# Another order of the first 42 feed-forward tasks in a fused attention and feed-forward kernel, with filler products in more places

## The chip, the cores and the metric

The kernel runs on one core of a Trainium2 chip. The metric is the device time of one execution in microseconds (us), as a median of several runs.

## What is computed

A recurrent attention (RWKV) runs over 4 batches, 8 heads and 768 positions with head size 48. Its output, 3072 tokens of 384 numbers, goes through two matrix products with a gelu between them.

```python
def _attn_ref(r, k, v, w, u):
    for t in range(S):
        kt, vt, rt, wt = (k[:, :, t], v[:, :, t], r[:, :, t], w[:, :, t])
        cur = np.einsum('bhd,bhe->bhde', u[None] * kt, vt)
        y[:, :, t] = np.einsum('bhd,bhde->bhe', rt, state + cur)
        state = wt[:, :, :, None] * state + np.einsum('bhd,bhe->bhde', kt, vt)
...
def _moe_ref(x, w_in, w_out):
    h = x @ w_in                                  # 3072x384 by 384x2048
    g = h * (1.0 / (1.0 + np.exp(-1.702 * h)))
    return (g @ w_out).astype(np.float32)         # 2048x384
```

## The kernel before

The 3072 tokens are 24 chunks of 128 (six for each batch). The attention of one chunk is a Python generator, `chunk(t)`, that is run in 13 steps. The feed-forward part is 6 groups of 4 chunks. A task is one group (or, for the first group's early tasks, half of it) with one of the 16 slices of the hidden dimension.

All instructions are issued in an order that is written out by hand: `RAMP` is a string of tokens, `do(token)` runs one token, and each engine gets its instructions in that order. An engine works its own list from front to back, so an instruction that must wait holds back all that stand behind it on the same engine. `RAMP` holds everything up to task 41; from task 42 on a fixed rule (`rest`) sets the order. The tokens are:

- `a5` runs the next step of chunk 5. This text calls them a5.1 to a5.13. Steps 1 to 3 are VectorE scans and the product `kq` (lines 330 to 341); 4 is four TensorE transposes and a ScalarE copy; 5 is `rku` on VectorE (line 356; line 359 to 361 from chunk 8 on); 6 is small TensorE products (`ps_d`, line 368) and 7 the ScalarE scaling of `am` from them; 8 is the TensorE products `ps_u`; 9 is the state update (lines 406 to 412); 10 the masked copies into `am` (line 415), which also give two PSUM banks back; 11 and 12 the TensorE products `ps_y` with a one-element copy between them (line 448); 13 moves `ps_y` into `x`, the input of the feed-forward part.
- `l5` issues loads of chunk 5, `m5` squares a scan's result on ScalarE (line 277), `f3` issues the load of weight piece 3, and `w3` runs one of four steps of its conversion: two ScalarE passes, two VectorE passes (lines 256 and 259), the high part on ScalarE, the low part on VectorE (line 267, tiles `l0` to `l11`).
- `g9`, `h9`, `y9` are task 9: first product (TensorE, tile `ph`), gelu (two ScalarE passes, then `gl` on VectorE, line 522), second product (TensorE, tiles `po`, line 540 to 542; the third of each three matmuls reads `gl`). Tasks 0 to 4 use one fp32 product in place of three (lines 497 and 537) and need only the first two conversion steps.
- `x1` copies attention rows into the third block of `x` of the first two chunks by six small DMAs (line 481), three from SyncE's queue and three from GpSimd's. `g0` reads them.
- `d6` sets 6 filler products: 128x512 bf16 matmuls of a constant tile `warm` with itself (line 305). They are issued by the next token that takes a PSUM bank, into that bank, ahead of its own work.

There are five banks for `bank(name)`, handed out in the order in which they were given back.

```python
BANKS = 5
...
def bank(name):
    i = free.pop(0)
    x = ps_a.tile([P, WIDE], F32, tag=f"bank{i}", name=name)
    while cold:
        times, n = cold.pop()
        for _ in range(times):
            T.matmul(..., warm, warm_b[:, 0:n], start=True, stop=True)
```

## Time and profile before

| | us |
|---|---|
| median of three runs | 501.91 (501.61 to 502.9) |
| span of the profiled execution, first to last instruction | 501.6 |
| TensorE busy | 489.3 (98%) |
| VectorE busy | 294.2 (59%) |
| ScalarE busy | 227.2 (45%) |

The profiled execution's own device time is not listed apart from the span. The median lies 0.3 us above the span, and the text takes these 0.3 us as what lies around it. Busy shares are means over the whole run. The VectorE and ScalarE work of the attention and of the weight conversion lies in the first third, where all three engines are close to full.

### The profile page before, as it was taken

The page shows a single profiled execution, that of the slowest core. Times are in us where ns is not written, and L with a number is a line of the kernel's source. Part 1 is how long each engine was busy: PE and PEld are TensorE (multiplying, and loading weights), DVE is VectorE, ACT ScalarE, POOL GpSimd, SP SyncE. Part 2 cuts the span into 40 slices and gives each one's busy share as a digit, 9 for nine tenths or more (in the row PEclk, how much of TensorE's full clock was granted, in tenths as well). Part 3 has the DMA queues.
Part 4 walks back from the last instruction along what each step waited for, and adds up shares of the span by engine and source line. Part 5 has one row for each costly group of instructions (what it writes and reads, how often), then busy time and mean ns, then how long its engine had stood idle before and what let it go on. Part 6 is the DMA issues. An engine that isn't in the chain of part 4 may idle for free.

```text
span 501.6 us, 11866 instructions
## 1 busy us (share of the span) xinstructions
PE 489.3 (98%) x5036; PEld 405.8 (81%) x5036; DVE 294.2 (59%) x502; ACT 227.2 (45%) x526; POOL 15.4 (3%) x48
## 2 busy tenths in 40 slices
PE   8989999999999999999999999999999999999996
PEld 4668999887887888888888888888888878888884
DVE  8889999989898314765655555655655521111211
ACT  2889899775444324432342442342442332322221
POOL 2001000001001000000001000001000001000000
PEclk9989999999999999999999999999999999999999
DMA  7884988056532500261104171104040001100001
GB/s 200 259 214 138 221 263 226 23 151 185 173 83 55 136 0 3 95 190 48 48 3 126 45 208 49 51 1 126 23 138 1 1 1 31 64 0 0 1 0 70
DMA packets 26508, 45.82 MB, mean 91 GB/s; under 512 B 3952, under 2 KB 17712, under 8 KB 26448
## 3 DMA queue, kind: packets, MB, share of 16 engines
q1 hardware_dynamic: 25472, 42.94, 30.5%
q0 software_dynamic: 864, 1.66, 1.4%
q8 instruction: 41, 0.67, 0.6%
q10 hardware_dynamic: 112, 0.39, 0.3%
q14 instruction: 19, 0.16, 0.1%
HBM read 38.00 MB, written 4.72 MB: 85 GB/s over the span
## 4 chain that ended last, share of the span: by engine, by line
PE 87%; DVE 8%; DMA 2%; issue 1%; ACT 1%; SPq 0%; DVEq 0%; ACTq 0%
PE po L540 12%; PE ph L502 12%; PE ph L504 12%; PE ph L503 12%; PE po L542 12%; PE po L541 12%; PE ps_y L438 2%; PE ps_y L425 2%; PE ps_u L402 2%; PE ph L497 2%; PE ps_u L398 2%; DMA wkr_t<-in_wkr 2%; PE ps_t L348 2%; PE po L537 1%; DVE lp L330 1%
## 5 line engine op out<-in xcount | busy, mean ns | idle before, releaser
L522 DVE TENSOR_TENSOR gl<-gf,gh 128x512 fp32r<-128x512 f32 (+1 forms) x101 | 65.7, 650 | 158.2 <-ACT gf L520 157.2
L519 ACT ACTIVATE gh<-ph 128x512 fp32r<-128x512 f32 (+1 forms) x101 | 57.1, 566 | 204.9 <-PE ph L504 193.8
L502 PE MATMUL ph<-x,h 128*128 128x512 f32 (+1 forms) x303 | 115.6, 382 | 0.7 <-DVE am L415 0.7
L504 PE MATMUL ph<-x,l 128*128 128x512 f32 (+1 forms) x303 | 113.4, 374 | 0.0
L540 PE MATMUL po<-gh,h 128*128 128x512 f32 (+1 forms) x297 | 113.3, 381 | 0.0
L503 PE MATMUL ph<-x,h 128*128 128x512 f32 (+1 forms) x303 | 113.2, 373 | 0.0
L542 PE MATMUL po<-gl,h 128*128 128x512 f32 (+1 forms) x297 | 111.2, 374 | 1.2 <-DVE gl L522 1.2
L541 PE MATMUL po<-gh,l 128*128 128x512 f32 (+1 forms) x297 | 110.9, 374 | 0.0
L502 PEld LDWEIGHTS ph<-x,h 128*128 128x128 f32 x303 | 57.0, 188 | 10.8 <-PE po L542 0.9
L542 PEld LDWEIGHTS po<-gl,h 128*128 128x128 f32 x297 | 55.9, 188 | 12.0 <-DVE gl L522 1.9
L504 PEld LDWEIGHTS ph<-x,l 128*128 128x128 f32 x303 | 57.0, 188 | 10.4
L503 PEld LDWEIGHTS ph<-x,h 128*128 128x128 f32 x303 | 57.1, 188 | 9.6
L540 PEld LDWEIGHTS po<-gh,h 128*128 128x128 f32 x297 | 55.9, 188 | 10.4
L541 PEld LDWEIGHTS po<-gh,l 128*128 128x128 f32 x297 | 56.0, 188 | 9.3
L520 ACT ACTIVATE gf<-ph 128x512 f32<-128x512 f32 (+1 forms) x101 | 56.7, 562 | 4.6 <-DVE gl L522 4.6
L330 DVE TENSOR_TENSOR_SCAN lp<-wkr_t,d1r 112x516 f32<-112x516 f32 x24 | 29.4, 1226 | 1.0 <-DMA wkr_t<-in_wkr 1.0
L341 DVE TENSOR_TENSOR kq<-wkr_t,lp 112x1024 f32<-112x1024 f32 x24 | 29.3, 1221 | 0.9 <-PE ps_y L438 0.6
L335 DVE TENSOR_TENSOR_SCAN lp<-wkr_t,d1f 112x516 f32<-112x516 f32 x24 | 29.5, 1229 | 0.5
L350 ACT COPY kt<-ps_t 128x448 f32<-128x448 f32 (+1 forms) x24 | 12.7, 530 | 34.4 <-PE ps_t L348 34.4
L277 ACT ACTIVATE junk<-lp 112x1032 bf16<-112x1032 f32 x24 | 25.5, 1063 | 0.0
L438 PE MATMUL ps_y<-kq,mid 64*64 64x64 f32 (+3 forms) x384 | 22.9, 218 | 0.8 <-ACT mid L448 0.4
L481 POOL DMA_DIRECT2D x<-x x18 | 9.0, 507 | 380.1 <-DVE x L272 269.2
(101 smaller groups left out, 517.5 us busy)
## 6 DMA issues: line engine op xcount, KB each, us to landing
st<-in_w_out SPq DMA_DIRECT2D x6, 1024.0 KB, 6.0
rk_t<-in_vrk SPq DMA_DIRECT2D x16, 384.0 KB, 4.3
st<-in_w_in SPq DMA_DIRECT2D x6, 896.0 KB, 8.6
v_t<-in_vrk SPq DMA_DIRECT2D x24, 192.0 KB, 3.7
out_t<-ob SPq DMA_DIRECT2D x15, 256.0 KB, 2.3
wkr_t<-in_wkr SPq DMA_DIRECT2D x18, 192.0 KB, 3.2
wkr_t<-in_wkr SPq DMA_DIRECT2D x36, 96.0 KB, 3.4
wkr_t<-in_wkr SPq DMA_DIRECT2D x5, 577.9 KB, 4.8
```

The source lines that it names most:

```text
L330: V.tensor_tensor_scan(li[:, ::-1], w1[:, ::-1], d1r.rearrange("r p c -> r (p c)")[:, ::-1], 0.0, op0=ALU.mult, op1=ALU.add)
L335: V.tensor_tensor_scan(pm, w0, d1f.rearrange("r p c -> r (p c)"), 0.0, op0=ALU.mult, op1=ALU.add)
L438: T.matmul(ps[b][head(h), p], from_[head(half), p * D + OFF * h : p * D + HB], qf[head(half), p, blocks[b]], start=False, stop=p == PAIRS[ ...
L502: T.matmul(ph, h_, xs[i][:, 0, c, cs], start=c == 0, stop=False)
L503: T.matmul(ph, h_, xs[i][:, 1, c, cs], start=False, stop=False)
L504: T.matmul(ph, l_, xs[i][:, 0, c, cs], start=False, stop=c == NM - 1)
L519: A.activation(gh, ph, AF.Gelu_apprx_sigmoid, scale=1.0 / W_SCALE)
L520: A.activation(gf, ph, AF.Gelu_apprx_sigmoid, scale=1.0 / W_SCALE)
L522: V.tensor_tensor(gl, gf, gh.bitcast(F32), op=ALU.subtract)
L540: T.matmul(o, h_, gh, start=first, stop=False, skip_group_check=True)
L541: T.matmul(o, l_, gh, start=False, stop=False, skip_group_check=True)
L542: T.matmul(o, h_, gl, start=False, stop=f == NF - 1, skip_group_check=True)
```

## The change

Only the string `RAMP` changes. Of its tokens other than the fillers each one occurs as often as before, so the work of every engine is the same; the place of many of them is another. The filler products go from 52 in 6 groups to 78 in 12 groups (14 tokens; two of the groups are filled by two tokens). What `rest` issues from task 42 on is the same. The first lines:

```diff
 RAMP = """
-l0 M l1 l0 a0 a0 a0 d26 a0 l0 a1 a0 d6 a0 f0 m0 a0 a0 l2 a1 l1 a1 l2 a0 a1 m1 a1 d6 a1 l3 a1 a0 a2 a1 a0 a1 a0 a1 w0
-l3 a2 a1 a0 a2 a3 d5 a2 a1 a1 f1 w1 f2 x1 a2 a3 d4 a2 a3 a2 a2 l4 a3 a2 a3 d5 a3 w0 f3 a3 a3 a2 a3 m2 a3 g0 h0 g1 w2
...
+d31 l0 a0 l1 a0 l0 a0 a0 m0 M a0 d3 a1 l0 a1 a0 a0 f0 l2 a1 d3 a0 d5 a0 a1 m1 d6 l2 a1 l1 a0 a2 a1 d3 a1 a1 a2 a1 a0
+a0 d5 l3 a2 a1 w0 d3 a2 a0 f1 f2 a1 d4 a1 d2 a3 l3 a2 a3 w1 a1 a2 x1 d4 l4 a2 a2 a3 a3 d5 w0 a3 a3 m2 a3 d3 g0 a2 a2
+a3 g1 f3 w1 h0 d1 l4 a3 w2 a3 a2 w2 h1 a2 f4 a2 a3 a4 g2 w3 a3 y0 w3 w2 y1 w0 a3 g3 g4 h2 h3 f5 w3 y2 h4 w0 y3 s0 y4
...
```

The number of filler products ahead of each piece of work, in TensorE's order, was 26 (transposes a0.4), 6 (a0.6), 6 (a1.6), 5 (a2.4), 4 (a2.6), 5 (a3.6). It is now 31 (a0.4), 3 (a0.6), 3 (a0.8), 5 (a1.4), 6 (a1.6), 3 (a1.8), 8 (a2.4), 6 (a2.6), 4 (a2.8), 5 (a3.6), 3 (`g0`) and 1 (a2.11).

TensorE around the first feed-forward product, before. `ps_d` is a3.6, `ps_u_527` and `ps_u_528` are a3.8, the six `ph` matmuls are `g0` and `g1` (three fp32 products each), and `ps_y_586` is a2.11.

```order
L368 MATMUL ps_d<-hm,rku 128x2 x4
L398 MATMUL ps_u_527<-v_t_84,kt 64x48
L398 MATMUL ps_u_527<-v_t_84,kt 48x48
...
L402 MATMUL ps_u_528<-kq 64x64
L497 MATMUL ph<-l_384,l_351 128x256 x6
L425 MATMUL ps_y_586<-am,v_t_86 48x64
```

The same place in the changed kernel, where a3.8 is `ps_u_558` and `ps_u_559`:

```order
L368 MATMUL ps_d<-hm,rku 128x2 x4
L305 LDWEIGHTS warm
L305 MATMUL ph<-warm 128x512
...
L497 MATMUL ph<-l_386,l_367 128x256 x3
L398 MATMUL ps_u_558<-v_t_84,kt 64x48
...
L402 MATMUL ps_u_559<-kq 64x64
L402 MATMUL ps_u_558<-kq 64x64
L497 MATMUL ph<-l_386,l_367 128x256 x3
```

`g0` now stands ahead of a3.8, behind three fillers, and a3.8 stands between `g0` and `g1`.

VectorE around the low part of weight piece 6 (`l6`, conversion step w6.4), before. `h11` with `st_844` is w6.2, `sf` and `mid` are a4.9, `am` is a4.10, `rku` a5.5, the `gl` rows are the tasks 12 and 13, and `st_857` with `h10` is w7.2.

```order
L259 SCALAR_TENSOR_TENSOR h11_952<-h11_952,st_844 128x1024
L522 TENSOR_TENSOR gl_1033<-gf_1031,gh_1032 128x256
...
L412 TENSOR_TENSOR sf1_88<-ps_u1_878,mid0_90 112x192
L267 TENSOR_TENSOR l6_1042<-h11_952,h6_1037 128x1024
L415 COPY_PREDICATED am_867<-after_102,ps_u0_877 128x256
...
L356 TENSOR_TENSOR rku_1063<-wkr_t1_83 112x512
L522 TENSOR_TENSOR gl_1077<-gf_1075,gh_1076 128x256
L256 SCALAR_TENSOR_TENSOR st_857<-st_857 128x1024
L259 SCALAR_TENSOR_TENSOR h10_1028<-h10_1028,st_857 128x1024
```

The same place in the changed kernel, where the `gl` rows are the tasks 12, 13 and 14 and `st_864` is w7.2's:

```order
L259 SCALAR_TENSOR_TENSOR h11_941<-h11_941,st_856 128x1024
...
L412 TENSOR_TENSOR sf1_88<-ps_u1_958,mid0_90 112x192
L522 TENSOR_TENSOR gl_1072<-gf_1070,gh_1071 128x256
L415 COPY_PREDICATED am_891<-after_102,ps_u0_957 128x256
...
L522 TENSOR_TENSOR gl_1127<-gf_1125,gh_1126 128x256
L356 TENSOR_TENSOR rku_1132<-wkr_t1_83 112x512
L522 TENSOR_TENSOR gl_1136<-gf_1134,gh_1135 128x256
L256 SCALAR_TENSOR_TENSOR st_864<-st_864 128x1024
L259 SCALAR_TENSOR_TENSOR h10_1055<-h10_1055,st_864 128x1024
L267 TENSOR_TENSOR l6_1150<-h11_941,h6_1102 128x1024
```

`l6` moved back past a4.10, a5.5, the whole of w7.2 and one more `gl`.

VectorE around the `gl` of task 25, the last of the first group, before. `am` is a8.7, `x` is a7.13, `lp` is a9.2 and `kq` a9.3.

```order
L383 TENSOR_TENSOR am<-same,s 128x256 x2
L272 TENSOR_TENSOR x<-ps_y_1771,x 112x4x64
L272 TENSOR_TENSOR x<-ps_y_1772,x 112x4x64
L335 SCALAR_TENSOR_TENSOR lp<-wkr_t_83,d1f 112x516
L341 TENSOR_TENSOR kq<-wkr_t_83,lp 112x1024
L522 TENSOR_TENSOR gl<-gf,gh 128x512
L359 TENSOR_TENSOR rk_t<-rk_t 128x384
```

The same place in the changed kernel (lines 408 to 412 are a8.9):

```order
L383 TENSOR_TENSOR am<-same,s 128x256 x2
L272 TENSOR_TENSOR x<-ps_y_1802,x 112x4x64
L272 TENSOR_TENSOR x<-ps_y_1803,x 112x4x64
L335 SCALAR_TENSOR_TENSOR lp<-wkr_t_83,d1f 112x516
L522 TENSOR_TENSOR gl<-gf,gh 128x512
L408 TENSOR_TENSOR sf_88<-sf_88,lp 112x192
...
L341 TENSOR_TENSOR kq<-wkr_t_83,lp 112x1024
```

The product `kq` of a9.3 went behind `gl` and behind a8.9.

## Rows read from the trace of the kernel before

**Rows 1.** The page: busy us, share of the span and instructions of each engine.

```profile
PE 489.3 (98%) x5036; PEld 405.8 (81%) x5036; DVE 294.2 (59%) x502; ACT 227.2 (45%) x526; POOL 15.4 (3%) x48
```

**Rows 2.** Stretches of 20 us: length, busy of five engines, granted clock, DMA share, GB/s.

```profile
60.00:80.00 20.00, 19.32 (x199) 18.96 (x199) 19.24 (x28) 17.93 (x43) 0.00 (x0) 1.00 0.74 222
...
180.00:200.00 20.00, 20.00 (x151) 16.50 (x150) 5.40 (x10) 5.58 (x11) 0.00 (x0) 1.00 0.01 1
```

**Rows 3.** Short stretches around the first feed-forward products, same columns.

```profile
26.00:28.00 2.00, 1.57 (x26) 0.94 (x15) 1.79 (x5) 1.97 (x6) 0.18 (x1) 1.00 1.13 212
28.00:30.00 2.00, 1.38 (x10) 0.97 (x8) 1.97 (x3) 2.00 (x9) 0.00 (x0) 1.00 1.05 215
...
31.00:32.00 1.00, 0.67 (x20) 0.51 (x13) 0.90 (x4) 1.00 (x5) 0.00 (x0) 0.93 0.91 113
32.00:33.00 1.00, 1.00 (x4) 0.82 (x3) 0.90 (x4) 1.00 (x2) 0.00 (x0) 0.50 0.45 162
...
35.00:36.00 1.00, 1.00 (x5) 0.64 (x3) 0.62 (x1) 1.00 (x2) 0.00 (x0) 0.86 0.65 224
```

**Rows 4.** TensorE (PEld: weight loads) in order of time: start, length, instruction, idle before.

```profile
1.14 7.46 PE L305 MATMUL ps_t<-warm 128*128 128x512 bf16 x26 [1.14 <-DVE warm L119]
...
4.53 3.57 PEld L305 LDWEIGHTS <-warm 128*128 128x128 bf16 x17 [0.28 <-issue]
...
9.39 0.57 PE L348 MATMUL ps_t<-ident,kq 112*128 112x112 f32 x4 [0.79 <-DVE kq L341]
...
19.24 0.68 PE L438 MATMUL ps_y<-kq,mid 64*64 64x64 f32 x8 [0.36 <-ACT mid L448]
...
31.62 4.51 PE L497 MATMUL ph<-l,l 128*128 128x256 f32 x12 [0.33 <-DVE am L415]
36.06 0.69 PE L425 MATMUL ps_y<-am,v_t 64*48 64x64 f32 x32
```

**Rows 5.** VectorE's first long wait, in a0.9.

```profile
14.84 0.36 DVE L412 TENSOR_TENSOR sf<-ps_u,mid 112x192 f32<-112x192 f32 x1 [1.25 <-ACT mid L406]
```

**Rows 6.** The DMAs of `x1`: issue; then KB each and median us to landing.

```profile
24.30 1.88 SPq L481 DMA_DIRECT2D l<-l  x3
...
x<-x SPq DMA_DIRECT2D x3, 32.0 KB, 2.3
l<-l SPq DMA_DIRECT2D x3, 16.0 KB, 6.5
```

**Rows 7.** TensorE in order of time: its waits behind 36 us, and some neighbours.

```profile
72.67 0.36 PE L502 MATMUL ph<-x,h 128*128 128x256 f32 x1 [0.68 <-DVE am L415]
...
75.77 0.39 PE L502 MATMUL ph<-x,h 128*128 128x256 f32 x1
...
81.37 0.28 PE L540 MATMUL po<-gh,h 128*128 128x256 f32 x1
81.49 0.28 PE L541 MATMUL po<-gh,l 128*128 128x256 f32 x1
82.09 0.39 PE L542 MATMUL po<-gl,h 128*128 128x256 f32 x1 [0.32 <-DVE gl L522]
...
123.19 0.39 PE L541 MATMUL po<-gh,l 128*128 128x512 f32 x1
124.49 0.50 PE L542 MATMUL po<-gl,h 128*128 128x512 f32 x1 [0.91 <-DVE gl L522]
...
153.18 0.69 PE L425 MATMUL ps_y<-am,v_t 64*48 64x64 f32 x32 [0.46 <-DVE am L415]
```

**Rows 8.** VectorE in order of time.

```profile
74.93 1.22 DVE L259 SCALAR_TENSOR_TENSOR h<-h,st 128x1024 int32<-128x1024 int32 x1
...
122.61 1.23 DVE L341 TENSOR_TENSOR kq<-wkr_t,lp 112x1024 f32<-112x1024 f32 x1
```

**Rows 9.** Waits of VectorE between 36 and 165 us: total, times, longest.

```profile
DVE mid L409 <- PE ps_u L402: 2.1, 3, 1.1
DVE mid L448 <- PE ps_y L438: 1.6, 2, 1.1
```

## The prediction

> **What bounds the kernel now.** I read the page first. TensorE is busy for 489.3 of 501.6 us, VectorE for 294.2 and ScalarE for 227.2 [rows 1]. So TensorE's list sets the end, and there are two ways to gain: fewer instructions in it, or less time in which it waits or runs slowly. The change adds instructions (26 fillers), so it can only gain by the second.

> The 20 us stretches say where that time lies. From 180 to 200 us TensorE has no gap (20.00 of 20.00) and VectorE is idle for three quarters. From 60 to 80 us TensorE misses 0.68 us, and VectorE (19.24) and ScalarE (17.93) are nearly full [rows 2]. So the first 160 us are a three-engine relay with little room, and what follows is TensorE alone. All tokens are the same but the fillers, so what is won or lost up to task 42 arrives at the end one for one.

> The busy share hides something. From 32 to 33 us TensorE counts as busy for 1.00 of 1.00 at a granted clock of 0.50, the lower of its two levels; the fall begins within the row from 31 us (0.93) and ends within the one from 35 us (0.86), with two more rows at 0.50 between [rows 3]. The loss is 0.07 + 3 x 0.50 + 0.14 = 1.7 us, and the 12 fp32 matmuls of `g0` and `g1` pay it: 4.44 us from their start at 31.62 to the next row at 36.06 [rows 4]. Ahead of the fall TensorE was busy for only 1.57 and 1.38 of 2 us, and 0.67 of 1 [rows 3].

> Then I listed the waits of TensorE behind 36 us. There are four of size: task 15's first product at 72.67 (released by the masked copy of a4.10, which gives its PSUM bank back), `y16` at 82.09 and `y25` at 124.49 (both for `gl`), and a11.11 at 153.18 (for a11.10) [rows 7]. The idle column is too small, since a matmul of 0.28 us is followed by the next after 0.12 (81.37, 81.49): `y16` lost 82.09 - 81.49 - 0.12 = 0.48, and by the same 0.16 task 15 lost 0.68 + 0.16 = 0.84 and `y25` 0.91 + 0.16 = 1.07 (from 123.19 to 124.49 less 0.23). For a11.11 I keep the 0.46 of its row. Together 2.85 us.

> **The change, part by part.** *Start.* A filler costs 3.57 / 17 = 0.21 us at the full clock [rows 4]. The first 26 run from 1.14 to 8.60, and the transposes a0.4 start at 9.39 after 0.79 of idle time for `kq`. Five more end 5 x 0.21 = 1.05 later, at about 9.65 by the last one's end; a next instruction overlaps that end by 0.16, so a0.4 starts at about 9.5, 0.1 late. Against that, `rku` of a0.5 now stands ahead of chunk 1's scan on VectorE, so a0.6 need not wait for it, ScalarE gets through a0.7 about 0.6 earlier, and VectorE's wait in a0.9 (1.25 us at 14.84 [rows 5]) falls to about 0.6. Then the fillers ahead of a0.8, a1.4, a1.6 and a1.8 come (17 in place of 6, 2.3 us), of which the relay hides most. I walked TensorE's list with the durations of the same steps in this trace and get a0.12 at 19.7 in place of 19.24 [rows 4]: 0.5 late.

> *To the first feed-forward products.* From a0.12 to a2.11 both orders hold the same real work of TensorE. Fillers in it go from 14 to 27: 13 x 0.21 = 2.8 us. They lie where TensorE was idle (0.43, 0.62 and 0.33 us in the three rows from 26 to 32 us, 1.4 in sum [rows 3]), and if they keep the clock up, 1.7 us of slow running go. By this account a2.11 moves by +0.5 + 2.8 - 1.4 - 1.7 = +0.2 us. The walk along the chain gives more, because idle time ahead of 26 us is filled too and a3.8 moves between `g0` and `g1`: a3.6 at 30.2, three fillers, `g0` at 31.85, a3.8 at 33.15, `g1` at 34.1, one filler, a2.11 at 35.65 in place of 36.06, that is -0.4. I take -0.4, since the walk sees the waits one by one, and keep +0.2 as the other end.

> *Task 15's wait.* In the bank list of the new order task 15 gets the bank of a5.4, which ScalarE frees early; a4.10's goes to a5.6. The 0.84 go.

> *A new wait.* `g16` is the first product that reads `l6`, in its third matmul. TensorE has the same real work ahead of `g16` in both orders, so it arrives there at 75.77 [rows 7] - 0.84 - 0.4 = 74.5 and wants `l6` at 74.8. VectorE now makes `l6` behind w7.2, which ended at 74.93 + 1.22 = 76.15 [rows 8] with `l6` already counted ahead of it; with one more `gl` (0.42 like any of that width, less 0.1 of overlap) and 0.4 of lead that is 76.1. Cost: 1.3 us. This is the price of moving `l6` back; its bounds are 0 (if VectorE gains an earlier start from its shorter waits) and 1.7 (no lead).

> *`y16`.* Two more first products and `h17` now lie ahead of it, 18 matmuls at 0.12 or 2.2 us of cover for `gl` of task 16. The 0.48 go.

> *`y25`.* The `kq` of a9.3 (1.23 us at 122.61 [rows 8]) no longer stands ahead of `gl`, which is then ready 1.2 us earlier, about when TensorE asks. The 1.07 go. Its transposes a9.4 are late by the same amount, but they now stand behind `g26`, which covers them.

> *a11.11.* It no longer follows a10.11 directly; feed-forward products lie between. The 0.46 go.

> Sum: -0.4 - 0.84 + 1.3 - 0.48 - 1.07 - 0.46 = -1.95 us, from 501.6 to 499.65 in span, and with the 0.3 us between span and median 499.9 us. Moves of loads I cost at nothing: no chunk load or weight piece is asked for later by more than it was early, and SyncE's weight loads of pieces 1 and 2 now stand ahead of a load that had to wait.

> [...]

> **The rivals.** *The waits come back elsewhere, or the clock falls all the same.* VectorE has 0.76 us free between 60 and 80 us [rows 2]. A TensorE that is 2 us earlier asks for `gl` earlier, and a product that now just makes it will wait. If the clock also falls at some other gap, 1.7 us go again. With either of these 499.9 becomes about 501.6. For it: the tight engines; against it: at the two hand-overs that I checked VectorE's own order became better.

> *VectorE gains too.* Between 36 and 165 us it waits 2.1 us for `ps_u` and 1.6 us for the copy of line 448, both for TensorE [rows 9], because products of the attention stand behind feed-forward products. The new order puts several of them ahead (a8.11 ahead of `y26`). If half of these 3.7 us goes, and TensorE is held by VectorE there, another 1.9 us go: 498.0.

> *Slower: the DMAs of `x1` come late.* a1.13 now stands behind a weight conversion on ScalarE, so `x1` is issued at about 27.1, 2.8 us later than 24.30 [rows 6]. Three issues take 1.88, so the last leaves some 1.3 after the first. With the 6.5 us to landing that they took then, the last lands at 34.9, while the last third of `g0` wants it at 31.85 + 0.86 = 32.7. TensorE waits 2.2 us, and the idle time brings the fall of the clock (1.7): 499.9 + 3.9 = 503.8. With the 2.3 us of the later `x` copies [rows 6] it lands at 30.7 and nothing waits. It decides at 4.3 us to landing. Against it: the 2 MB of weight pieces that those DMAs shared the queues with are now asked for earlier.

> **How the numbers follow.** As summed (499.9): 0.42, with a range of its own from 498.7 to 501.2. VectorE gains too (498.0): 0.17. Waits or the slow clock come back (501.6): 0.24. Late `x1` (503.8): 0.17. A measurement of this kernel can tell about 0.3%, 1.5 us, from no change: faster is below 500.4, slower above 503.4. Of the first case three quarters lie below 500.4 (0.32), which with the second and a little of the third gives 0.52 for faster; late `x1` is slower in most of its cases (0.14); 0.34 is left for no change. The range leaves out 2 in 10: the far half of the second case and most of the late `x1`, so 497.5 to 502.8.

> **What would show it.** Right: a granted clock of 1.00 from 5 us on; a0.12 near 19.7, `g0` near 31.9 and a2.11 near 35.7; no wait at task 15, `y16` and `y25`; a wait of about 1.3 us of `g16`'s third matmul for VectorE's line 267; task 42's first product about 2 us earlier. Wrong: `g0` waiting for the DMAs of line 481, a clock of 0.50 in any stretch, or new TensorE waits for line 522 that add up to what the four old ones cost.

## The result and the profile after

| | us |
|---|---|
| before, median of 6 runs | 502.27 (501.61 to 502.9) |
| changed, median of 6 runs | 508.02 (506.46 to 511.18) |
| ratio, with 95% interval | 1.0112, [1.0086, 1.0139] |
| span of the profiled execution | 509.5, its own time 511.18: the slowest of the six |

The change makes the kernel slower by 1.1%, about 5.7 us, where 499.9 was forecast. A run's time is 1.7 us above its span, not 0.3 as I had reckoned. So before's profiled execution, with its span of 501.6, took about 503.3 us and was some 1.0 above before's median; the changed kernel's was 3.2 above its own.

The changed kernel's page, answering [rows 1], and TensorE in order of time, answering [rows 4]:

```profile
PE 498.2 (98%) x5062; PEld 409.5 (80%) x5062; DVE 294.4 (58%) x502; ACT 227.0 (45%) x526; POOL 15.4 (3%) x48
```

```profile
19.78 0.67 PE L438 MATMUL ps_y<-kq,mid 64*64 64x64 f32 x8 [0.24 <-ACT mid L448]
...
32.56 1.46 PE L497 MATMUL ph<-l,l 128*128 128x256 f32 x6
...
35.03 1.56 PE L497 MATMUL ph<-l,l 128*128 128x256 f32 x6
...
36.74 0.46 PE L425 MATMUL ps_y<-am,v_t 64*48 64x64 f32 x16
...
41.30 0.27 PE L438 MATMUL ps_y<-kq,sf 64*64 64x64 f32 x1 [2.01 <-issue]
```

a0.12 is where the walk had it (19.78 against 19.7). Against the walk `g0` is 0.7 late (32.56 for 31.85) and a2.11 is 1.1 late (36.74 for 35.65). The fall of the clock at `g0` and `g1` is gone. Then comes something that no row of before has: at 41.30, in the middle of a3.11, TensorE had stood for 2.01 us and waited for nothing that the trace names. Such a gap, ended by `issue` in the rows, is called a stop below. Behind it the clock falls; the short stretches, as [rows 3]:

```profile
42.00:43.00 1.00, 1.00 (x3) 0.83 (x4) 0.51 (x2) 0.97 (x2) 0.00 (x0) 0.58 1.06 246
43.00:44.00 1.00, 1.00 (x4) 0.72 (x3) 0.00 (x0) 1.00 (x2) 0.00 (x0) 0.50 1.06 143
...
121.00:122.00 1.00, 1.00 (x5) 0.90 (x4) 0.90 (x4) 1.00 (x6) 0.00 (x0) 0.50 1.06 317
```

There are two falls of 3.4 us ahead of the end in this execution, from 42.2 and from 120.7 us, with 1.7 us lost in each. The second has no stop in front of it. What `g0` has ahead of it shows on ScalarE (`w1.1` is the row of L253, a1.13 those of L462 behind it):

```profile
23.86 0.13 ACT L448 COPY mid<-ps_y 1x1 f32<-1x1 f32 x1
26.80 1.20 ACT L253 ACTIVATE st<-st 128x1024 int32<-128x1024 uint32 x1 [2.81 <-DMA st<-in_w_out]
27.88 1.20 ACT L254 ACTIVATE h<-st 128x1024 f32<-128x1024 f32 x1
...
29.04 0.39 ACT L462 ACTIVATE l<-ps_y 112x256 f32<-112x256 f32 x1
```

The load of piece 1 was issued at 15.49 in place of 18.91, and `w1.1` got it 1.5 us later than before (26.80 against 25.25). a1.13 waits behind it, and `x1` is issued at 29.92. The DMAs from SyncE's queue then landed in 1.9 us (median), not in 6.5 [rows 6]:

```profile
29.92 1.89 SPq L481 DMA_DIRECT2D l<-l  x3
```

```profile
l<-l SPq DMA_DIRECT2D x3, 16.0 KB, 1.9
```

The waits of TensorE from 36 to 165 us that the view lists (total, times, longest); the four of [rows 7] are gone, but for 0.2 us of L542:

```profile
PE ps_y L438 <- issue: 2.0, 1, 2.0
PE ps_y L438 <- ACT mid L448: 0.8, 3, 0.3
PE ph L504 <- DVE l L267: 0.4, 1, 0.4
PE po L542 <- DVE gl L522: 0.2, 1, 0.2
```

**Where the time went.** For each trace I took the start of every real matmul of TensorE (no filler) and subtracted the real work before it, each matmul at the median interval to the next one that its line and shape have in before. What is left is lost: waits, fillers, slow clock. It is given when 18, 70, 90, 130 and 200 us of real work are done (in before at 43, 99, 121, 166 and 239 us). The rows e1 to e14 are experiments of the next section; each row is one execution.

```
lost, us            18    70    90   130   200
before            24.9  28.6  31.3  36.2  38.5
changed           30.2  33.8  39.7  44.0  46.3
e1  same again    27.4  30.9  36.8  41.1  43.4
e3                25.2  31.4  36.9  40.6  42.9
e4                25.2  28.8  32.8  37.1  39.4
e5                24.5  26.7  29.7  34.5  36.8
e9                28.4  32.0  37.8  41.5  43.8
e10               26.4  30.0  35.5  39.8  42.0
e14               26.1  29.8  33.7  38.0  40.2
```

Of the 7.8 us between the two profiled executions 5.3 arise in the first stretch and 3.2 in the third, 0.6 come back in the fourth. From 18 to 70 both orders lose the same (3.7 and 3.6). In the first stretch 0.7 are there by a2.11 (36.74 against 36.06); the stop (2.0) and the fall behind it (1.7) make most of the rest. In the third the second fall makes 1.7, and waits that no row of before has make 1.2 (`Not seen at all`, below).

### The profile page after: what moved, and what is told of

It is laid out like the page before. It is cut to its first block, busy times and chain, and to the rows that moved or that the text cites. A ratio compares the mean times of both kernels' runs of the same rounds, so it can differ in the third digit from the quotient of the medians.

```text
span 509.5 us, 11912 instructions
## 1 busy us (share of the span) xinstructions
PE 498.2 (98%) x5062; PEld 409.5 (80%) x5062; DVE 294.4 (58%) x502; ACT 227.0 (45%) x526; POOL 15.4 (3%) x48
## 4 chain that ended last, share of the span: by engine, by line
PE 89%; ACT 4%; DVE 2%; DMA 2%; issue 2%; ACTq 0%
PE po L540 13%; PE ph L502 12%; PE ph L504 12%; PE po L542 12%; PE po L541 12%; PE ph L503 12%; PE ps_y L438 3%; PE ps_y L425 2%; DMA st<-in_w_out 2%; PE ps_u L402 2%; PE ps_u L398 2%; PE ps_t L305 2%; PE ps_t L348 2%; ACT am L378 1%; PE po L564 1%
## 5 line engine op out<-in xcount | busy, mean ns | idle before, releaser
L542 PE MATMUL po<-gl,h 128*128 128x512 f32 (+1 forms) x297 | 111.5, 376 | 0.2 <-DVE gl L522 0.2
L542 PEld LDWEIGHTS po<-gl,h 128*128 128x128 f32 x297 | 56.2, 189 | 10.6 <-DVE gl L522 0.4
L438 PE MATMUL ps_y<-kq,mid 64*64 64x64 f32 (+3 forms) x384 | 24.3, 221 | 1.6 <-ACT mid L448 1.3
L438 PEld LDWEIGHTS ps_y<-kq,mid 48*48 48x48 f32 (+3 forms) x384 | 19.2, 129 | 4.8 <-ACT mid L448 2.0
```

The source lines that it names most:

```text
L438: T.matmul(ps[b][head(h), p], from_[head(half), p * D + OFF * h : p * D + HB], qf[head(half), p, blocks[b]], start=False, stop=p == PAIRS[ ...
L542: T.matmul(o, h_, gl, start=False, stop=f == NF - 1, skip_group_check=True)
```

## The experiments

The first theories: A, the load of piece 1 lands late and holds ScalarE, with `x1` and `g0` behind it; B, the 26 fillers lie on TensorE's path; C, the loss is made by the later order; D, stops and falls of the clock. Ratios are against runs of before beside each group of experiments, on the same chip; before's median there was 503.15 (e1 to e4), 502.48 (e5 to e8), 503.42 (e9 to e12) and 503.17 (e13 to e16).

**e1: the changed kernel again.** 

> The changed kernel as it is, for a second profile. The first one has two stretches of granted clock 0.50 (from 42.2 and from 120.7 us) and a stop of TensorE of 2.0 us at 39.07 for which the trace names nothing. Theory A (the load of weight piece 1 lands late and holds ScalarE at the first step of its conversion, with a1.13, a2.7 and so g0 behind it): that chain belongs to the order and shows again, with w1.1 on ScalarE starting at 26.8 +- 0.3 us and a2.11 at 36.7 +- 0.5, before any fall of the clock. If the stop at 39.07 and the falls are what makes it slower (rival D), they are here again at the same places; if they are missing here and the time is still 505 us or more, they are not the cause.

Measured: 508.2 us, ratio 1.0105 [1.0044, 1.0166]. `w1.1` started at 25.09 without a wait, so the late landing is not a property of the order alone. The stop at a3.11 was 0.31 us and no clock fell ahead of the end; yet the profiled run took 508.24. In its place there was a stop of 1.59 us at 122 us, in a chain of small products (below).

**e2: the first step of w1 later.**

```diff
-a3 w1 a1 a2 x1 d4 l4 a2 a2 a3
+a3 a1 a2 x1 d4 l4 a2 w1 a2 a3
```

> The changed order with one token moved: the first step of w1 stands behind a2.7 on ScalarE and no longer ahead of a1.13. Theory A: a1.13 and a2.7 no longer wait for the load, x1 is asked for at about 27 us in place of 29.9, g0 starts at about 31.9 in place of 32.6, and 1 to 3 us of the 5.8 come back: 504 to 506 us. Theory B (26 more fillers on TensorE's path) and theory C (the loss is made by the order behind 50 us): no change, 507 to 509 us.

Measured: 507.6 us, 1.0087 [1.0057, 1.0117]. `x1` was issued at 25.77, 4.1 us sooner, and `g0` started at 32.50, no sooner: it now waited for those DMAs, 6.7 us behind their issue; in before they took 6.5 (median) to land [rows 6].

```profile
32.50 0.70 PE L497 MATMUL ph<-l,l 128*128 128x256 f32 x2 [0.42 <-DMA l<-l]
```

Theory A falls as the cause: its chain is real, but to take `w1.1` out of it moved `g0` by 0.06 us.

**e3 and e4: order and fillers apart.** e3 has before's order and the changed kernel's 78 fillers ahead of the same steps; e4 the other way round.

> The order of before with the 78 fillers of the changed kernel ahead of the same pieces of work. Theory B: 506 to 508 us, since 26 fillers at 0.21 us are 5.5 us. Theories A and C: 501.5 to 503.5 us, since the fillers lie mostly in idle time and only the order of the other tokens does harm.

> The order of the changed kernel with the 52 fillers of before ahead of the same pieces of work. Theory B: 502 to 503.5 us. Theories A and C: 506.5 to 509 us; the granted clock may fall at more places, since there are fewer fillers in the first 35 us.

Measured: e3 508.94 us, 1.0132 [1.0078, 1.0186]; e4 508.28, 1.0112 [1.0074, 1.015]. Each half alone costs as much as both, so neither B nor C can be read as a sum. For e3 the table says how: nothing is lost by 43 us (25.2 against 24.9), and the loss comes later, from one wait for a weight load with a fall behind it and from two stops. For e4 it does not: its profiled execution was the fastest of its four (504.28), and the other three, of 508.2 to 510.4 at a lower mean clock (0.987 to 0.991 against 0.998), have no trace. TensorE in e1, e2 and e3, around the stops:

```profile
123.88 0.21 PE L438 MATMUL ps_y<-kq,sf 48*48 48x64 f32 x1 [1.59 <-issue]
```

```profile
124.48 0.26 PE L438 MATMUL ps_y<-kq,sf 48*48 48x64 f32 x1 [2.93 <-issue]
```

```profile
118.63 0.50 PE L542 MATMUL po<-gl,h 128*128 128x512 f32 x1 [1.26 <-issue]
...
123.96 0.25 PE L438 MATMUL ps_y<-kq,sf 48*48 48x64 f32 x1 [1.02 <-issue]
```

In three kernels, of two orders, the stop comes behind the same count of TensorE's instructions: 3265, with weight loads, matmuls and the semaphore waits between them counted. That of a3.11 comes behind 1217, and e3's first behind 3009. These counts lie 256 apart or a multiple (256, 2048). Such a place is called a border here, and the 256 instructions between two borders a block. One DMA queue carries something in portions that fit (queue, packets, MB, share), before and then changed:

```profile
q8 instruction: 41, 0.67, 0.6%
```

```profile
q8 instruction: 42, 0.69, 0.6%
```

```
border at instruction; TensorE enters the block before it, packet starts, lands; border reached, goes on
before   3265   116.81  118.34  119.22   121.38  121.60
changed  1217    34.48   38.59   39.61    39.07   41.30
e1       3265   117.85  121.18  122.42   122.08  123.88
e2       3265   117.10  121.82  122.88   121.33  124.48
e3       3009   112.42  116.06  117.03   116.98  118.63
e3       3265   118.63  121.42  122.41   122.71  123.96
```

At the five stops TensorE goes on 1.5 to 1.7 us after the packet's landing. (In the traces up to e12 there are 17 gaps over 0.4 us, from one start to the next, at such borders; the time from landing to going on is 1.4 to 1.7 us in 16 of them.) In before the packet landed 2.2 us ahead of the border. So there is a new theory, of code loading: the order and the number of instructions ahead decide which small products (32 pairs in 0.69 us at 36.06 [rows 4]) share a block of 256, and a block that is run through faster than the next one is brought stops TensorE. The changed kernel ran through the block ahead of 1217 in 4.6 us (34.48 to 39.07), and the packet landed 5.1 us after the entry: a stop. Before took 4.6 us for its block ahead of 3265 (116.81 to 121.38), and the packet landed after 2.4: none.

**e5: four local moves on before.** a4.10 ahead of w6.4; a6.1 behind `h16`; a9.3 behind `h25`; `g31` between a10.11 and a11.11.

```diff
-h12 w6 a4 w6 y11 a4 a5 a5
+h12 w6 a4 a4 w6 y11 a5 a5
...
-y13 a6 h16 y14
+y13 h16 a6 y14
...
-x7 a9 g25 y24 h25 y25 a9
+x7 g25 y24 h25 a9 y25 a9
...
-a10 a11 l13 a10 a10 a11 y30
+a10 g31 a11 l13 a10 a10 a11 y30
```

> The order of before with four local moves alone, one for each wait that the prediction wanted gone: a4.10 ahead of w6.4 (task 15), a6.1 behind h16 (y16), a9.3 behind h25 (y25), g31 between a10.11 and a11.11. If the prediction's terms are real by themselves, the four waits go from the trace and the sum 0.84 + 0.48 + 1.07 + 0.67 = 3.1 us is gained: 498.5 to 500.5 us. If the waits only turn up elsewhere on TensorE (the rival of the prediction), 501.5 to 503.5 us.

Measured: 501.78 us, 0.998 [0.995, 1.0011]: not to be told from before. The waits of task 15 and `y16` are gone from the trace (18 to 70: 2.2 us lost in place of 3.7). That of `y25` turned up at the next second product, and there was a stop of 1.68 us at 1217:

```profile
38.26 0.21 PE L438 MATMUL ps_y<-kq,mid 64*64 64x64 f32 x1 [1.68 <-issue]
...
129.37 0.50 PE L542 MATMUL po<-gl,h 128*128 128x512 f32 x1 [0.76 <-DVE gl L522]
```

**e6 and e9: before, only its code shifted.** e6: `d26` becomes `d20 e32`. These narrow fillers were not 64 but 256 columns wide, and a0.12 came 2.1 us late. e9 has tiny ones, with `d26` as `e30 d22` (its line numbers are 3 higher from there). Both move the code by 52 instructions. What makes the fillers of e9 tiny:

```diff
+                if n:
...
+                else:
+                    T.matmul(x[0:64, 0:64], warm[0:64, 0:64], warm[0:64, 0:64], start=True, stop=True)
```

> Before, with 6 of its first 26 fillers replaced by 32 narrow ones (64 columns), so that 26 more pairs of weight load and matmul stand ahead of everything, as in the changed kernel, in about the same time; the order of all else is that of before. Theory of code loading (TensorE's instructions arrive in packets of 16 KB, 256 instructions, and TensorE stops at a packet's border when the next has not landed some 1.5 us earlier): at the border behind 3265 visible instructions, near 122 us, TensorE stops for 1 to 3 us, with nothing that it waits for, as in the order of before with the 78 fillers; 503.5 to 506.5 us. If the borders play no part: no such stop, and 502 to 503.5 us.

> Before, with 4 of its first 26 fillers replaced by 30 tiny ones (64 columns of 64 rows, some 0.03 us each), so that TensorE's code is moved by 52 instructions as in the changed kernel; a0.4 and a0.12 should start within 0.3 us of before (the narrow fillers of the first shift were 256 wide and made the start 2 us late). Theory of code loading: stops at the borders 3009 and 3265 again, 1 to 3 us in sum, and a fall of the clock behind some of them: 504 to 507 us. If the shift of the first try cost its time by the late start alone: 502 to 503.5 us and no stop.

Measured: e6 508.02 us, 1.0134 [1.0098, 1.017]; e9 507.14, 1.0066 [1.0035, 1.0097], with a0.12 at 19.66. Both stop at 3009 and 3265; for e9 both stops were forecast from the count alone, for e6 the one at 3265. TensorE in e6 and in e9:

```profile
115.50 0.39 PE L541 MATMUL po<-gh,l 128*128 128x512 f32 x1 [1.20 <-issue]
...
120.82 0.21 PE L438 MATMUL ps_y<-kq,sf 48*48 48x64 f32 x1 [0.91 <-issue]
```

```profile
119.25 0.39 PE L544 MATMUL po<-gh,l 128*128 128x512 f32 x1 [1.49 <-issue]
...
124.84 0.21 PE L441 MATMUL ps_y<-kq,sf 48*48 48x64 f32 x1 [1.18 <-issue]
```

52 instructions more at the head, with the order of before, cost 3.7 us by the medians of e9, and 1.8 to 4.9 by the interval. The stretch with the two stops (70 to 90) loses 5.8 in e9 in place of before's 2.7. In e9's profiled execution another 4 us went at 29.6 to 33.8: there, too, `w1.1` had waited 4.27 us for its load.

```profile
28.95 1.16 ACT L253 ACTIVATE st<-st 128x1024 int32<-128x1024 uint32 x1 [4.27 <-DMA st<-in_w_out]
```

How much of the 3.7 is such late loads and not the stops isn't shown, since the other executions have no trace.

**e7 and e10: the changed kernel, its borders moved.** e7 has 138 of the 256-wide fillers for 39 of the others ahead of a1.8; e10 `d31` as `e114 d16`, with tiny ones.

> The changed kernel with 39 of its fillers ahead of a1.8 replaced by 138 narrow ones, which moves every later packet border by 198 instructions, that is 58 back in terms of the 256. Theory of code loading: the stop near 122 us (and that at a3.11) is gone, since the border behind the dense stretch now falls into a feed-forward product; 504 to 506.5 us. Theory that the order alone makes the loss: 507 to 509 us. Should the narrow fillers take longer than I reckon (0.06 us each), a0.12 is late, and the time has to be read from there.

> The changed kernel with 15 of its first 31 fillers replaced by 114 tiny ones: the code moves by 198 instructions, the start should stay (a0.12 within 0.4 us of 19.8). Theory of code loading: no stop at a3.11 and near 122 us, the runs lie closer together, and the median is 504.5 to 506 us: half of the loss is the stops, the other half stays (early fillers that nothing hides, new waits for line 448). If the stops are a mere symptom of other waits: 507 to 509 us.

Measured: e7 511.42 us, 1.0191 [1.0167, 1.0216], with no stop at all, but a0.12 at 26.08: 6.3 us late by the fillers' width; taken off one for one, an estimate, that is 505.1. e10: 506.33, 1.0056 [1.0032, 1.0079], no stop. Its waits from 36 to 165 us:

```profile
PE ps_y L441 <- ACT mid L451: 0.8, 3, 0.3
PE ph L507 <- DVE l L267: 0.4, 1, 0.4
PE po L545 <- DVE gl L525: 0.2, 1, 0.2
```

The interval lies apart, by little, from the changed kernel's first one (from 1.0086), but not from e1's (from 1.0044). By the ratios about half of the loss is the stops and what they bring; by the plain medians (506.33 against 508.02) it is 1.7 of 5.7 us. The other part is there without any stop.

**e8: the load of piece 2 behind `x1`.** 

> The changed kernel with the load of weight piece 2 behind x1 in place of right behind the load of piece 1. Theory A (piece 1 lands late since both share the DMA engines): piece 1 lands before 25.5 us in place of 26.8, w1.1 on ScalarE starts by then, x1 is asked for at 28.6 in place of 29.9 and g0 starts at about 31.6 in place of 32.6; 506 to 507.5 us, w2.1 may be late in its place. If piece 1 lands at 26.8 all the same, the sharing is not the reason.

Measured: 512.57 us, 1.0207 [1.0175, 1.024]. Piece 1 was there by 24.29, `x1` issued at 27.32, `g0` at 32.18. That is what sharing would give, but it does not show it: piece 1 took 6.8 us from issue to landing here, and 6.7 in e1, where piece 2 stood right behind it; in the changed kernel's first trace it took 11.3. And `g0` wins only 0.4 us, and stops at 1217 and 3265 with a fall behind each are back.

**e11: e5 with its code moved by 208** (`e120 d10`). 

> The order of before with the four local moves, and 16 of the first 26 fillers replaced by 120 tiny ones (code moved by 208 instructions), so that by the durations of its blocks the border at a3.11, where this order stopped for 1.7 us, falls into slower code. Theory of code loading: no stop behind 30 us, 499.5 to 501 us, faster than before by 0.3 to 0.5%. Otherwise 501.5 to 502.5 us, as without the shift.

Measured: 503.83 us, 1.0002 [0.9974, 1.003]. The stop at a3.11 is gone, a new one (1.37 us, at 705) stands at 21.5, with a fall of the clock. I put that down to the denser code at the head, which e11 alone does not show.

**e12: e10 with before's fillers up to a1.8** (`e123 d15`, and 6 ahead of a0.6 and of a1.6, none at a0.8, a1.4, a1.8). 

> The changed kernel with the same borders as with the second shift, but with before's number of fillers up to a1.8 (12 in place of 25 behind a0.4, and fewer at the head). If the fillers ahead of a0.8, a1.4 and a1.8 are on TensorE's path, as the lost time at that point says (17.6 us in the changed kernel, 15.2 before), the median is 1.5 to 2.5 us below that of the second shift: 502.5 to 504 us. If the relay hides them, as the prediction had it, both are the same.

Measured: 508.9 us, 1.009 [1.0054, 1.0126], and not faster: without those fillers TensorE stops for 1.43 us at 705. The question whether they are hidden stays unanswered by it; a wide filler also stretches its block, by the 0.21 us that it takes [rows 4].

**e13, e14, e15: the other half.** e13 is e10 with a5.12 and a6.12 behind the next products, e14 is e10 without 13 of the fillers from a2.4 on (and `e128 d15` at the head), e15 has both. The diff of e13:

```diff
-g23 a5 a5 a7 a6 h23 a6
+g23 a5 a7 a6 h23 a5 a6
...
-y22 a6 a5 a6 a7 l9 a8 a7 a7 l8
+y22 a6 a5 a7 l9 a8 a7 a7 a6 l8
```

> The changed kernel with its packet borders moved (as with the tiny fillers before), and with a5.12 and a6.12 put behind the next products, so that they no longer stand right behind a5.11 and a6.11 and wait for the one-element copy of line 448 between them (0.46 and 0.44 us in the traces of the new order, none in before). If these two waits are a part of the other half of the loss, they go, and the median falls by 0.5 to 1 us, from 506.3 to 505.3 to 505.8 us; if VectorE and not TensorE sets the time there, the wait turns up at the next product and nothing changes.

> The changed kernel with its packet borders moved, without the 13 fillers that it has more than before from a2.4 on (8, 6, 4, 5, 3, 1 become 5, 4, 0, 5, 0, 0). By the lost time at g5 (26.4 us there, 24.9 before, of which 1.7 a slow clock) some 2 us of the fillers are not hidden. If so and the clock holds: 504 to 505 us. If the idle time that they fill brings the slow clock back in the first 45 us: 506 to 507 us, and the fillers are worth what they cost.

> Both of the two: copies apart and 13 fillers fewer, on the changed kernel with its borders moved. If both theories hold: 503 to 504.5 us, which would leave the new order level with before at best; if neither: 506 to 507 us.

Measured: e13 509.2 us, 1.0101 [1.0058, 1.0144]; e14 505.49, 1.0035 [1.0009, 1.0061]; e15 507.8, 1.0067 [1.0036, 1.0098]. In e13 the two waits for the copy go, and TensorE waits longer at the next transposes:

```profile
118.82 0.72 PE L351 MATMUL ps_t<-ident,kq 112*128 112x112 f32 x3 [1.41 <-DVE kq L344]
```

VectorE sets the time there. e15 has the same wait. The 13 fillers look like 0.8 us, but the intervals of e10 and e14 overlap.

**e16: e9 with the loads of chunk 10 later** (`l10 l10` behind `x7`, the first two steps of chunk 10 behind `y26`). 

> The order of before with its code moved by 52 instructions (which stopped at the borders 3009 and 3265, near 117 and 123 us, for 1.8 and 1.4 us), and the loads of chunk 10 put behind x7 in place of ahead of it, so that the DMA engines have less to do from 113 to 120 us; a10.1 and a10.2 go behind y26 for it. If the packets of code are late because the DMA engines are full: the packets for these two borders start within 1.5 us of the entry into the block before, and both stops shrink below 0.7 us. If they are late whatever the DMA engines do: they start 2.5 to 3.5 us after it as before, and the stops stay.

Measured: 504.81 us, 1.0025 [0.9989, 1.0061]. The stops shrink to 0.94 and 0.34 us; the packets started 3.1 and 2.3 us after the entry (3.5 and 2.4 in e9).

```profile
117.41 0.40 PE L544 MATMUL po<-gh,l 128*128 128x512 f32 x1 [0.94 <-issue]
...
122.19 0.21 PE L441 MATMUL ps_y<-kq,sf 48*48 48x64 f32 x1 [0.34 <-issue]
```

Half a yes: less load traffic and smaller stops in one execution of each, but not the prompt packets that I expected, and the intervals of the times of e9 and e16 overlap.

## Why the prediction was wrong, step by step

Forecast were 499.9 us, with a range from 497.5 to 502.8; measured were 508.02. Two things failed: the price of added and moved instructions, and the term of -0.4 up to the first feed-forward products. The first is not enough by itself: e10, which has no stop, still lies above the range with 506.33.

**"The change adds instructions (26 fillers), so it can only gain by the second."** The step that failed most. I costed fillers by their 0.21 us and took the rest of TensorE's list as the same work. By the stops at 1217, 3009 and 3265 the list also comes in blocks of 256, and both its length ahead of a place and its density there changed. e9 shows the price with the order untouched (3.7 us, late loads included), e10 takes the stops away (from 1.0112 to 1.0056).

**To the first feed-forward products, -0.4.** This term was mis-sized. In e10, without stops, 18 us of work are done 1.5 us later than before (26.4 against 24.9), and before's figure contains a fall of 1.7. The 1.7 us in it I took from one execution: twelve of before's 87 later runs have a mean clock of 1.00 and cannot have had it, with spans of 499.9 to 501.5, so against the median only a part of it was there to win. How large a part isn't shown. And fillers, loads and moves cost more than the walk said. How much each, e12 and e14 don't settle.

**"Moves of loads I cost at nothing."** Not settled. The load of piece 1 was issued 3.4 us earlier and landed later, but e1, the same program, had it in 6.7 us in place of 11.3: it varies from execution to execution by more than the move. For `g0` it made at most 0.7 us.

**Task 15, `y16`.** Right: both waits are gone, and in e5, by themselves, the stretch from 18 to 70 is 1.5 us shorter (0.84 + 0.48 = 1.32 forecast). **`g16`'s wait for `l6`.** Right in place and cause, too large:

```profile
80.86 0.28 PE L503 MATMUL ph<-x,h 128*128 128x256 f32 x1
81.55 0.39 PE L504 MATMUL ph<-x,l 128*128 128x256 f32 x1 [0.41 <-DVE l L267]
```

That is 0.69 - 0.12 = 0.57 of 1.3; VectorE gained the rest on TensorE, as the lower bound allowed. Yet from 18 to 70 only 0.1 was won in sum, since other small waits came in (the first rival, in kind). My terms for this stretch (-0.84, -0.48 and +1.3) also add up to nothing: that the sum fits is luck, two errors that cancel.

**`y25`, a11.11.** Gone from the trace, but worth less: both lie between 90 and 130, and that stretch gives 0.6 of 1.07 + 0.46 = 1.53. In e5 `y25`'s wait moved on to the next second product.

**Not seen at all:** a5.12 stands right behind a5.11 and a6.12 close behind a6.11 in the new order, and TensorE waits for the copy between them (0.46 and 0.44 us):

```profile
117.26 0.43 PE L438 MATMUL ps_y<-kq,mid 48*48 48x64 f32 x8
...
117.93 0.44 PE L438 MATMUL ps_y<-kq,mid 64*64 64x64 f32 x8 [0.24 <-ACT mid L448]
```

Their rows stood in the order; I had looked at the places where waits went, not where new neighbours came. With 0.34 at the transposes behind them they make the third stretch 1.2 us longer (e4, e14).

**The rivals.** Late `x1` named the right place on ScalarE and the right direction, but it costs `g0` at most 0.7 us, not 2.2, and is not what decides (e2). The slow clock did come back: in the changed kernel's trace once behind a stop (from 42.2 us) and once without one (from 120.7). "VectorE gains too" did not come: from 36 to 165 us it waits for `ps_u` and `ps_y` 4.8 us in the changed kernel's trace and 4.3 in before's.

**The falls of the clock.** Of the 13 falls ahead of the end in the traces up to e12, 10 come with an idle stretch of TensorE of 1.3 us or more. Before's, and those at 120.7 us in the changed kernel and at 117.2 us in e10, come without one: TensorE's longest wait in the 3.5 us ahead of them is 0.71, 0.24 and 0.24 us.

**Open:** what is left in e14, without stops and without 13 of the fillers (0.35%, interval 0.09 to 0.61); the fall at 120.7 us; and whether full DMA engines are why the packets start late.

## What to carry to other kernels

Where TensorE runs many short instructions, as here, look for stops that come behind a fixed count of them. If there are some, count the instructions between two borders (256 here), and ask what the shortest block lasts against the time that its successor needs to come (4.6 against 5.1 us at the stop of the changed kernel). A single execution's clock fall is not a term of the median: 12 of 87 runs of before cannot have had the 1.7 us. Look for it in the spans of several runs before counting on its going. And a filler is not free time filled: it moves every border behind it. In e9, 52 instructions more at the head came with two stops (1.49 and 1.18 us), and the median rose by 3.7 us, late loads included.

## What the runs showed of the hardware

- Up to 150 us, a code packet started at the median 0.6 us after TensorE entered the block ahead of its border when the DMA engines were under 20% busy within 1 us of that (some 40 blocks, at most 2.0 us), and 1.8 us after it when they were over 80% busy (115 blocks, up to 6.0). This is a correlation over the traces up to e12: six of the 17 gaps at borders had less than 80% (the least 41%, in e6), and e16 shows it only in part.
- In two executions of one program the same load of piece 1 took 11.3 us from issue to landing (waited for until 26.80) and 6.7 us (not waited for at 25.09).
- The first rise of the clock came between 4.0 and 7.2 us in these traces, and at 4.6 and 7.0 in two executions of one program. The late one put a0.12 about a microsecond back (20.97 in e1 against 19.78).
- A stop need not bring a fall of the clock: TensorE stood for 1.59 us in e1 and for 1.68 us in e5 without one.
